# Moving the third and fourth quarter of w_out into the first pass, and x's second reading ahead of w_in

## The chip, the cores and the metric

The kernel runs on one core of one Trainium2 chip. The metric is the time of one execution on the device in microseconds (us); lower is better. The core has TensorE (PE in the rows; its weight loads are PEld), VectorE (DVE), ScalarE (ACT), GpSimd (POOL) and SyncE (SP), which issues nearly all DMAs. Each engine works through its own instructions in the order in which the program writes them.

## What is computed

The input x has 8 sequences of 3072 tokens with 256 channels. Three stages follow one another:

```python
X = np.fft.fft(np.fft.fft(x, axis=1), axis=2).real          # 24576 tokens x 256
logits = X @ phi                                            # soft mixture of 8 experts, 32 slots
d = softmax of logits over all tokens; c = softmax over slots
slot_input = d.T @ X                                        # 32 x 256
slot_out[e] = np.maximum(slot_input[e] @ w1[e], 0) @ w2[e]  # w1: 8 x 256 x 1024, w2: 8 x 1024 x 256
Y = c @ slot_out
h = Y @ w_in                                                # w_in: 256 x 2048
out = (s * np.maximum(h, 0)**2 + b) @ w_out                 # w_out: 2048 x 256
```

w_in and w_out are float64 in memory; the kernel turns them into float32 itself.

## The kernel before, in words

**The stages.** The *first pass* reads x once, turned, in 24 pages of 1 MB (`load_x`, three to a sequence) and computes the logits' Fourier sums: `emit_v` (L381) multiplies a page with the projected table on TensorE into `vt`, ScalarE or VectorE copies that to `vts`, `turn_v` (L412) transposes it and copies it to `v`, and `emit_t` (L426) makes `tps` (for the last sequence `tpa` and `tpb`), which ScalarE copies to `tt`. For the last but one sequence these eight copies are put aside in `late_t` and written out after `emit_t`. Then come the logits (`lp`, L571), their maximum, the exponentials `dt` and `hp` (L651). The *second pass* (L829 on) reads x again in another order, 24 pages `xrt` (`load_xr`), and sums `slot_input` in `racc` (L726), two pages to a step, while VectorE, GpSimd and ScalarE make the second softmax (`c_steps`). Then the experts use w1 (L925) and w2 (L957), and last the feed-forward blocks (L1121, L1151, L1154), which make up most of the time.

**Pages.** The loaded tiles and several others live in pages of 8 KB per partition: 15 in `ring`, three and two more behind the first pass, two more in the second. `page` takes one and `drop` gives it back; a DMA into a page waits until its former content has been read. SP issues in order, so a load that waits holds up all loads behind it.

**w_out and w_in.** Each is loaded in four chunks of 1 MB. `wo_load(k)` (L194) takes a page for the raw float64 numbers, and for every second chunk also a page `wo` for float32 and a page `whl` for the two float16 parts that the blocks use. Its work is a list of small steps: four integer steps on VectorE (L154 to L166), a product (L174), a maximum (L224), four bias adds on GpSimd (L283), a scale (L206, L207) with two casts on ScalarE (L214), and two low parts on VectorE (L218), which wait for the casts. The raw page is given back with the product, the `wo` page with the odd chunk's last low part. `wi_load(k)` does the like for w_in with the first steps and the maximum.

**Who orders it.** Everything is written out by hand in one order per engine. A planner keeps rough times in `at` while it writes: `pump_a` (L320) takes loads from the string `ORDER` (x: a page of the first reading, w: a chunk of w_out, r: a page of the second reading, l and h: tables) as long as enough pages are free, and `fill` writes the small steps in where it believes VectorE to be idle:

```python
def fill():
    while side_step(at["pe"] + 0.7):
        pass
```

`side_step(0.0, True)` writes the next small step whatever the planner believes. Behind the first pass the loads stand in the list `todo`, and `pump` takes the next one when it has the pages it asks for (first entry of its tuple; third entry: that many in the first two pools).

Of the kernel before, what the change touches and what calls it, by code (L numbers as in the profile page):

```python
# [9 lines left out]
F16 = mybir.dt.float16  # L10
# [22 lines left out]
def tile_fft2__then__softmoe__then__act_relu2(  # L33
# [19 lines left out]
    P = 128  # L53
# [53 lines left out]
    todo = []  # L107
# [19 lines left out]
    def side_step(limit, any_time=False):  # L127

        met = set()
        for n, (c, lag, f, cost) in enumerate(side_work):  # L130
            start = max(at["dve"], side_at[c] + lag)
            if c not in met and (any_time or start < limit):
                side_work.pop(n)
                f()
                at["dve"] = side_at[c] = start + cost
                return True
            met.add(c)
        return False
# [53 lines left out]
    wo_rest = []  # L192

    def wo_load(k):  # L194
        if k % 2 == 0:
            t, kk = page([P, 8, D], F32, "wo")
            wo.append(t)
            wok.append(kk)
            whl.append(page([P, 8, 2, D], F16, "whl", 2)[0])
# [5 lines left out]
        def scale():  # L205
            nc.vector.tensor_scalar(out=top, in0=top, scalar1=1e-30, scalar2=1.0 / WMAX, op0=ALU.max, op1=ALU.mult)  # L206
            nc.vector.reciprocal(inv, top)  # L207
            if k < 2:
                cast()
# [18 lines left out]
        rest = [(0.0, lambda j=j: low(j), 0.65) for j in range(2)]  # L228
        if k > 1:
            steps[4:4] = wo_rest  # L230
            wo_rest[:] = [(0.0, cast, 0.0), *rest]
        else:
            steps += rest
# [3 lines left out]
    def wi_load(k):  # L237
# [9 lines left out]
        steps[4:4] = wo_rest  # L247
        wo_rest.clear()
# [55 lines left out]
    ORDER = "xxxwxxxxxxwxxxxxxxxxxxrllhhrr"  # L304
# [69 lines left out]
    with tc.tile_pool(name="xtp", bufs=1, side="right") as xtp, tc.tile_pool(name="vp", bufs=1, side="right") as vp, \  # L374
# [136 lines left out]
        while side_step(0.0, True):  # L511
            pass
        turn_v(2 * B - 2)
        emit_v(2 * B - 1)
        turn_v(2 * B - 1)
        nc.gpsimd.tensor_copy(ltabs[0][0][64:P], ltabs[0][0][0:64])
        nc.gpsimd.tensor_copy(ltabs[1][0][64:P], ltabs[1][0][0:64])
        emit_t(B - 1)
        load_xr()
# [291 lines left out]
    todo += [(1, load_xr)] * (left - 8)  # L811
    for k in (2, 3):
        todo += [(5 - 2 * (k - 1), doubles.pop(0)[1], 3 - k), (1, load_xr)]
    for k in range(4):
        todo += [(2 - k % 2, lambda k=k: wi_load(k), 1 - k % 2), (1, load_xr)]
    todo += [(1, load_xr)] * 2
# [18 lines left out]
    for n in range(NST + 2):  # L835
# [13 lines left out]
        for _ in range(2 if n >= 5 else 1 if n == 4 else 0):  # L849
            side_step(0.0, True)  # L850
        c_until(CR * n + CR / 2)
        for _ in range(2 if n >= 6 else 1 if n >= 4 else 0):
            side_step(0.0, True)
# [456 lines left out]
```

## Time and profile before

| | before |
|---|---|
| median of 3 runs | 1399.15 us (1397.02 to 1400.8) |
| the profiled execution | 1397.21 us, its span 1395.4 us |
| TensorE busy | 98% of the span |
| VectorE / ScalarE / GpSimd busy | 84% / 73% / 17% |

The profiled execution is one run; its span reaches from the first to the last instruction of the program, and 1.8 us of its time lie around the span. It lies 1.9 us below the median. All times below count from the span's start. A row of a timeline tells start, length, engine, line, operation and tiles of a group of like instructions, and in brackets how long the engine was idle before it and what released it.

### The profile page before, as it was taken

The numbers are of one execution on the slowest core, as the hardware profiler recorded it, in microseconds if no ns is written. First come the engines' busy times: TensorE is split into PE (matmuls) and PEld (weight loads), VectorE is DVE, ScalarE is ACT, GpSimd is POOL, SyncE is SP. The second block draws the span as 40 slices with busy tenths as digits, with TensorE's granted clock in tenths as the row PEclk, the third lists the DMA queues.
The fourth block names the chain that finished last, engine by engine and source line by source line (L and its number), as shares of the span: only waits on it lengthen the run. The fifth ranks groups of instructions, "written<-read, shape, count | busy, mean of one in ns | idle before, by whom it ended". The sixth has DMA issues, their size and how long they took to land.

```text
span 1395.4 us, 23097 instructions
## 1 busy us (share of the span) xinstructions
PE 1374.5 (98%) x9036; PEld 841.0 (60%) x9036; DVE 1165.6 (84%) x1477; ACT 1014.8 (73%) x1436; POOL 234.0 (17%) x287
## 2 busy tenths in 40 slices
PE   8989989999999999999999999999999999999998
PEld 6767545566666666666666666666666666666665
DVE  2447946998989898989899998989898989888886
ACT  2767325877778777778777777777777777777775
POOL 1227100121212121212121211111111111111110
PEclk9999999999999999999999999999999999999999
DMA  9997991101010101010101101010101010101000
GB/s 353 417 318 310 403 410 56 36 24 37 23 37 20 36 20 37 23 37 20 37 23 30 30 23 34 23 35 22 36 24 33 23 36 24 37 23 33 24 21 30
DMA packets 72382, 112.28 MB, mean 80 GB/s; under 512 B 33904, under 2 KB 59632, under 8 KB 64976
## 3 DMA queue, kind: packets, MB, share of 16 engines
q1 hardware_dynamic: 72144, 110.70, 23.2%
q8 instruction: 71, 1.16, 0.4%
q14 instruction: 39, 0.32, 0.1%
q0 software_dynamic: 128, 0.10, 0.0%
HBM read 78.48 MB, written 25.17 MB: 74 GB/s over the span
## 4 chain that ended last, share of the span: by engine, by line
PE 90%; DMA 8%; DVE 1%; SPq 1%; ACT 0%; issue 0%; ACTq 0%; DVEq 0%
PE op L1151 47%; PE op L1154 24%; PE fhp L1121 12%; DMA xb<-in_x_turned_dram 4%; PE racc L726 3%; DMA w2t<-in_moe_w_dram 1%; DMA xrt<-in_x_pages_dram 1%; DMA htab_t<-in_htab_dram 1%; PE vt L401 1%; PE hp L651 1%; PE dps L711 1%; PE eop L957 1%; SPq L1084 0%; PE tps L454 0%; DVE r L1127 0%
## 5 line engine op out<-in xcount | busy, mean ns | idle before, releaser
L1151 PE MATMUL op<-whl,rhl 128*128 128x512 f16 x3072 | 1025.3, 379 | 0.8 <-ACT rhl L1111 0.6
L1154 PE MATMUL op<-whl,rhl 128*128 128x256 f16 x3072 | 835.7, 273 | 0.0
L1126 ACT ACTIVATE r<-fhp,wsc 128x768 f32<-128x768 f32 (+1 forms) x513 | 461.4, 900 | 230.5 <-PE fhp L1121 229.4
L1127 DVE SCALAR_TENSOR_TENSOR r<-fhp,r 128x768 f32<-128x768 f32 (+1 forms) x513 | 488.5, 952 | 113.8 <-ACT r L1126 103.7
L1112 DVE TENSOR_TENSOR rhl<-r,rhl 128x768 f16<-128x768 f32 x511 | 506.2, 991 | 0.9 <-ACT rhl L1111 0.9
L1151 PEld LDWEIGHTS <-rhl 128*128 128x128 f16 x3072 | 300.5, 98 | 335.6 <-ACT rhl L1111 0.9
L1111 ACT CAST rhl<-r 128x768 f16<-128x768 f32 x511 | 420.2, 822 | 1.8 <-DVE r L1127 1.8
L1154 PEld LDWEIGHTS <-rhl 128*128 128x128 f16 x3072 | 300.6, 98 | 62.5 <-issue 0.3
L1166 POOL TENSOR_TENSOR ot<-ot,bias 128x256 f32<-128x256 f32 x189 | 137.7, 729 | 974.6 <-DVE ot L1164 974.6
L1121 PE MATMUL fhp<-ct,g 128*128 128x384 f16 x1024 | 250.5, 326 | 1.1 <-DMA g<-gs 0.8
L1121 PEld LDWEIGHTS <-g 128*128 128x128 f16 x1024 | 99.9, 98 | 69.0 <-issue 1.1
L1163 ACT ACTIVATE o<-op,small 128x256 f32<-128x256 f32 x189 | 89.6, 475 | 16.7 <-PE op L1154 16.7
L1164 DVE SCALAR_TENSOR_TENSOR ot<-op,small,o 128x256 f32<-128x256 f32 x192 | 91.6, 477 | 0.3
L401 PE MATMUL vt<-xb,phd 128*64 128x512 f32 (+3 forms) x288 | 48.8, 479 | 1.9 <-DMA xb<-in_x_turned_dram 1.8
L726 PE MATMUL racc<-xrt,dh 128*64 128x256 f32 x384 | 44.3, 382 | 0.7 <-ACT dh L716 0.7
L423 DVE COPY v<-vq 128x512 f32<-128x512 f32 (+1 forms) x15 | 8.4, 594 | 39.9 <-PE vq L419 39.9
L401 PEld LDWEIGHTS vt<-xb,phd 128*64 128x64 f32 x288 | 27.3, 139 | 20.8 <-issue 10.8
L726 PEld LDWEIGHTS racc<-xrt,dh 128*64 128x64 f32 x384 | 26.4, 137 | 21.2 <-issue 7.5
L468 ACT COPY tt<-tps 32x512 f32<-32x512 f32 x48 | 27.7, 576 | 6.5 <-PE tps L454 6.0
L410 ACT COPY vts<-vt 128x512 f32<-128x512 f32 (+1 forms) x15 | 8.0, 536 | 30.3 <-PE vt L401 30.1
L773 POOL TENSOR_TENSOR lg<-lg,rm 112x512 f32<-112x512 f32 x16 | 22.9, 1435 | 3.3 <-DVE rm L771 3.3
L755 POOL TENSOR_TENSOR lg<-et,lg 112x512 f16<-112x512 f32 x16 | 18.6, 1160 | 0.5 <-ACT lg L758 0.5
(230 smaller groups left out, 504.9 us busy)
## 6 DMA issues: line engine op xcount, KB each, us to landing
xb<-in_x_turned_dram SPq DMA_DIRECT2D x24, 1024.0 KB, 20.2
xrt<-in_x_pages_dram SPq DMA_DIRECT2D x24, 1024.0 KB, 13.8
out_dram<-ot SPq DMA_DIRECT2D x128, 128.0 KB, 1.7
w1t<-in_moe_w_dram SPq DMA_DIRECT2D x8, 1024.0 KB, 17.7
out_dram<-ot SPq DMA_DIRECT2D x128, 64.0 KB, 2.0
raw<-in_moe_w_out_dram SPq DMA_DIRECT2D x4, 1024.0 KB, 13.7
raw<-in_moe_w_in_dram SPq DMA_DIRECT2D x4, 1024.0 KB, 11.5
w2t<-in_moe_w_dram SPq DMA_DIRECT2D x4, 1024.0 KB, 19.3
```

What stands on the lines that cost most here:

```text
L401: nc.tensor.matmul(vt[64 * h:64 * h + 64, o:o + k, :], lhsT=phd[:, c, sg, :], rhs=turned(pg, c, i, k, rev), start=(c == 0 and m < 2), stop ...
L726: nc.tensor.matmul(raccs[acc][64 * h:64 * h + 64, :], lhsT=dh[:, m, g].rearrange("p j e -> p (j e)"), rhs=xr[k][0][:, g, t, :], start=(sum ...
L1111: nc.scalar.copy(a, r2)
L1112: nc.vector.tensor_tensor(out=l, in0=r2, in1=a, op=ALU.subtract)
L1121: nc.tensor.matmul(hp[k * split][:, k, :].rearrange("p (s b m) -> p s b m", s=2, b=B), lhsT=g16[:, f * P:(f + 1) * P], rhs=c, start=True, ...
L1126: nc.scalar.activation(out=r[:, k], in_=hp[i][:, k], func=AF.Relu, scale=wsc[:, 2, p:p + 1])
L1127: nc.vector.scalar_tensor_tensor(out=r2[:, k], in0=hp[i][:, k], scalar=0.0, in1=r[:, k], op0=ALU.max, op1=ALU.mult)
L1151: nc.tensor.matmul(op.rearrange("p h d -> p (h d)"), lhsT=a, rhs=w.rearrange("p h d -> p (h d)"), start=(f == 0), stop=False)
L1154: nc.tensor.matmul(op[:, 0, :], lhsT=l, rhs=w[:, 0, :], start=False, stop=(f == NFC - 1))
L1163: nc.scalar.activation(out=o1, in_=op[:, 1, :], func=AF.Copy, scale=qv)
L1164: nc.vector.scalar_tensor_tensor(out=ot, in0=op[:, 0, :], scalar=qv, in1=o1, op0=ALU.mult, op1=ALU.add)
L1166: nc.gpsimd.tensor_tensor(out=ot, in0=ot, in1=bias, op=ALU.add)
```

## The change

The third chunk of w_out is loaded in the first pass ahead of x's last four pages, the fourth behind x's last page, in place of one page of the second reading; in the second pass all remaining pages of x but four come ahead of w_in. `whl` may now lie in any pool. `side_step` gets a bound `below` on the chunk. The third chunk's casts come with its scale, the fourth's as a step of their own; the list `wo_rest`, which had delayed them, is gone. At the end of the first pass only steps of the first three chunks are written out where all were; the fourth chunk's steps follow one, two and two at three later places, and the last six in steps 1 and 2 of the second pass, where w_in's begin at step 6.

```diff
@@ -124,10 +124,12 @@
 
     side_at, raws, doubles = {}, [0], []
 
-    def side_step(limit, any_time=False):
+    def side_step(limit, any_time=False, below=9):
 
         met = set()
         for n, (c, lag, f, cost) in enumerate(side_work):
+            if c >= below:
+                continue
             start = max(at["dve"], side_at[c] + lag)
             if c not in met and (any_time or start < limit):
                 side_work.pop(n)
@@ -189,14 +191,12 @@
         for _ in range(k):
             nc.tensor.matmul(t, lhsT=ones[:, :t.shape[0]], rhs=ones[:, :t.shape[1]], start=True, stop=True)
 
-    wo_rest = []
-
     def wo_load(k):
         if k % 2 == 0:
             t, kk = page([P, 8, D], F32, "wo")
             wo.append(t)
             wok.append(kk)
-            whl.append(page([P, 8, 2, D], F16, "whl", 2)[0])
+            whl.append(page([P, 8, 2, D], F16, "whl")[0])
         w = wo[k // 2][:, 4 * (k % 2):4 * (k % 2) + 4, :]
         hl = whl[k // 2][:, 4 * (k % 2):4 * (k % 2) + 4]
         d = w.rearrange("p k d -> p (k d)")
@@ -205,7 +205,7 @@
         def scale():
             nc.vector.tensor_scalar(out=top, in0=top, scalar1=1e-30, scalar2=1.0 / WMAX, op0=ALU.max, op1=ALU.mult)
             nc.vector.reciprocal(inv, top)
-            if k < 2:
+            if k < 3:
                 cast()
 
         def cast():
@@ -225,12 +225,9 @@
             out=top, in_=d.rearrange("p (a n) -> p a n", a=2), axis=AX.X, op=ALU.max, apply_absolute_value=True), 1.15))
         steps.append((0.0, lambda: bias_add(k, d.rearrange("p (k d) -> p k d", d=D)), 0.0))
         steps.append((0.0, scale, 0.35))
-        rest = [(0.0, lambda j=j: low(j), 0.65) for j in range(2)]
-        if k > 1:
-            steps[4:4] = wo_rest
-            wo_rest[:] = [(0.0, cast, 0.0), *rest]
-        else:
-            steps += rest
+        if k == 3:
+            steps.append((0.0, cast, 0.0))
+        steps += [(0.0, lambda j=j: low(j), 0.65) for j in range(2)]
         side_at[k] = dma_ready()
         side_work.extend((k, *f) for f in steps)
 
@@ -244,8 +241,6 @@
         steps = double_steps(d, w_in[c * P:(c + 1) * P, 1024 * h:1024 * h + 1024], False)
         steps.append((0.0, lambda: nc.vector.tensor_reduce(
             out=wim4[:, k:k + 1], in_=d, axis=AX.X, op=ALU.max, apply_absolute_value=True), 1.15))
-        steps[4:4] = wo_rest
-        wo_rest.clear()
         side_at[4 + k] = dma_ready()
         side_work.extend((4 + k, *f) for f in steps)
 
@@ -301,7 +296,7 @@
     CR = 1.5
     WARM = 4
     LEAD, TOL, LT, LX, HX = 14.0, 0.5, 0, 0, 1
-    ORDER = "xxxwxxxxxxwxxxxxxxxxxxrllhhrr"
+    ORDER = "xxxwxxxxxxwxxxxxxxwxxxxwllhhrr"
     tpool = tc.alloc_tile_pool(name="tpool", bufs=1)
     doubles += [((3, 1, 3, 1)[k], lambda k=k: wo_load(k)) for k in range(4)]
 
@@ -508,14 +503,19 @@
         emit_t(B - 2)
         for f in late_t:
             f()
-        while side_step(0.0, True):
+        while side_step(0.0, True, 3):
             pass
         turn_v(2 * B - 2)
+        side_step(0.0, True)
         emit_v(2 * B - 1)
         turn_v(2 * B - 1)
+        for _ in range(2):
+            side_step(0.0, True)
         nc.gpsimd.tensor_copy(ltabs[0][0][64:P], ltabs[0][0][0:64])
         nc.gpsimd.tensor_copy(ltabs[1][0][64:P], ltabs[1][0][0:64])
         emit_t(B - 1)
+        for _ in range(2):
+            side_step(0.0, True)
         load_xr()
         keep_warm(psv.tile([P, 4 * P], F32, tag="vt", name="warm", bufs=2)[:, :P], WARM)
         for i in range(2):
@@ -808,12 +808,9 @@
         nc.sync.dma_start(out=w2t[e][:, c], in_=w2[e].rearrange("(p c) d -> p c d", p=P)[:, c])
 
     left = NS1 - len(xr) - sum(t[1] is load_xr for t in todo)
-    todo += [(1, load_xr)] * (left - 8)
-    for k in (2, 3):
-        todo += [(5 - 2 * (k - 1), doubles.pop(0)[1], 3 - k), (1, load_xr)]
+    todo += [(1, load_xr)] * (left - 4)
     for k in range(4):
         todo += [(2 - k % 2, lambda k=k: wi_load(k), 1 - k % 2), (1, load_xr)]
-    todo += [(1, load_xr)] * 2
     todo += [(1, lambda e=e: w1_load(e)) for e in range(8)] + [(1, lambda e=e: w2_load(e)) for e in range(4)]
     parts2 = [(e, 0) for e in range(4, 8)] + [(4, 3), (5, 3), (6, 3), (7, 1), (7, 4), (7, 5)]
     todo += [(h == 0, lambda e=e, h=h: w2_load(e, h)) for e, h in parts2]
@@ -846,10 +843,10 @@
             r_sum(n - 2, dhs[n - 2], 0)
         busy("dve", 0.6)
         c_until(CR * n)
-        for _ in range(2 if n >= 5 else 1 if n == 4 else 0):
+        for _ in range(2 if n > 5 or n in (1, 2) else 0):
             side_step(0.0, True)
         c_until(CR * n + CR / 2)
-        for _ in range(2 if n >= 6 else 1 if n >= 4 else 0):
+        for _ in range(2 if n > 5 else n in (1, 2)):
             side_step(0.0, True)
         at["pe"] += 4.9
         if n >= 2:
```

## Rows read from the trace of the kernel before

**Rows 1.** Stages: busy us (instructions) per engine, granted clock, DMA share, GB/s.

```profile
57.90:83.20 25.30, 25.30 (x175) 17.26 (x174) 5.02 (x9) 19.71 (x36) 4.40 (x4) 1.00 1.02 341
...
83.20:89.30 6.10, 3.86 (x86) 3.21 (x84) 2.43 (x4) 4.85 (x12) 4.56 (x4) 1.00 1.04 209
...
121.00:149.40 28.40, 27.08 (x222) 15.50 (x223) 23.38 (x38) 12.14 (x24) 18.32 (x18) 1.00 0.79 291
...
202.00:208.00 6.00, 2.89 (x24) 1.08 (x26) 0.21 (x1) 0.77 (x2) 0.00 (x0) 0.83 1.01 406
...
224.00:1395.40 1171.40, 1165.53 (x7170) 700.76 (x7166) 1047.51 (x1288) 909.91 (x1235) 180.83 (x227) 1.00 0.11 29
```

**Rows 2.** Timeline of PE from 186 to 222 us, the second expert matrix.

```profile
206.41 3.37 PE L957 MATMUL eop<-w2t,hT 128*32 128x256 f32 x26 [1.90 <-DMA w2t<-in_moe_w_dram]
...
210.29 1.93 PE L957 MATMUL eop<-w2t,hT 128*32 128x256 f32 x32
...
215.39 2.52 PE L957 MATMUL eop<-w2t,hT 128*32 128x256 f32 x32
```

**Rows 3.** Timeline of SP: issues at 141 and 208 us.

```profile
141.73 0.33 SPq L333 DMA_DIRECT2D xrt<-in_x_pages_dram  x1
...
208.95 0.33 SPq L808 DMA_DIRECT2D w2t<-in_moe_w_dram  x1
```

**Rows 4.** Issues at 126, 141 and 208 us: KB, us to landing.

```profile
xrt<-in_x_pages_dram SPq DMA_DIRECT2D x1, 1024.0 KB, 5.0
...
xrt<-in_x_pages_dram SPq DMA_DIRECT2D x1, 1024.0 KB, 7.6
...
w2t<-in_moe_w_dram SPq DMA_DIRECT2D x1, 128.0 KB, 7.7
```

**Rows 5.** What SP waited for until 240 us: total us, times, longest.

```profile
SPq L333 <- PE racc L726: 24.4, 8, 5.0
```

**Rows 6.** SP's issues of x from 46.8 to 54.9 us, and their landing.

```profile
46.86 7.81 SPq L296 DMA_DIRECT2D xb<-in_x_turned_dram  x4
...
xb<-in_x_turned_dram SPq DMA_DIRECT2D x4, 1024.0 KB, 20.0
```

**Rows 7.** Timeline of all engines at the end of the first pass.

```profile
74.83 3.65 PE L401 MATMUL vt<-xb,phd 128*64 128x512 f32 x16
...
80.50 4.69 ACT L466 COPY tt<-tps 32x512 f32<-32x512 f32 x8 [1.04 <-PE tps L454]
...
80.83 2.38 PE L401 MATMUL vt<-xb,phd 128*64 128x384 f32 x20
...
80.94 0.69 DVE L423 COPY v<-vq 128x512 f32<-128x512 f32 x1 [5.24 <-PE vq L419]
...
83.33 0.56 DVE L410 COPY vts<-vt 128x384 f32<-128x384 f32 x1 [1.70 <-PE vt L401]
...
83.94 0.55 PE L419 MATMUL vq<-ident,vts 128*128 128x128 f32 x3 [0.73 <-DVE vts L410]
...
85.07 1.16 PE L432 MATMUL tpa<-f_sb,v 128*128 128x128 f32 x8 [0.58 <-DVE v L423]
...
86.27 2.98 ACT L436 COPY tt<-tpa 32x256 f32<-32x256 f32 x8 [1.08 <-PE tpa L432]
...
89.30 0.97 PE L571 MATMUL lp<-tt,ltab 64*64 64x128 f32 x13 [0.93 <-ACT tt L436]
```

**Rows 8.** Chunk steps: ns of one, shortest, median and longest.

```profile
L214 ACT ACTIVATE whl<-wo,wsc x8: 705/722/737, 38.7 to 162.9; 128x512 f16<-128x512 f32 x8
...
L218 DVE SCALAR_TENSOR_TENSOR whl<-wo,wsc,whl x8: 742/746/753, 39.5 to 163.8; 128x512 f16<-128x512 f32 x8
...
L166 DVE TENSOR_SCALAR raw<-raw x8: 689/689/691, 32.6 to 182.9; 128x1024 uint32<-128x1024 uint32 x8
```

**Rows 9.** Timelines of ACT and POOL early in the second pass.

```profile
128.90 0.64 ACT L769 ACTIVATE lg<-lg 112x512 f32<-112x512 f32 x1
...
145.20 3.47 POOL L283 TENSOR_TENSOR bias<-bias,wo 128x256 f32<-128x256 f32 x4 [5.79 <-DVE wo L174]
```
## The prediction

> **What bounds the kernel now.** I read busy time by stage first, then who waits in the stages that are not full: TensorE's timeline, SP's issues and waits, the end of the first pass. From 224 us to the end TensorE is busy for 1165.5 of 1171.4 us [rows 1]: the feed-forward blocks run back to back, so whatever moves their start moves the end one for one. The change touches nothing behind that point; the question is when the blocks start.
>
> Before 224 us, TensorE has three faces. In the first pass, 57.9 to 83.2 us, it has no idle time at all [rows 1]. In the second pass it is nearly full too. But from 202 to 208 us it works 2.89 of 6 us [rows 1]: the second matrix of the experts (L957) waits for w2t, and its last group ends at 215.39 + 2.52 = 217.9 us [rows 2]. The last piece of w2 was issued at 208.95 us and landed 7.7 us later, at 216.65 [rows 3, 4]. So **the end of the loads** releases the blocks, 1.25 us before the last group ends.
>
> At the end the loads run without a gap, at 406 GB/s; from 121 to 149.4 us they move only 291 [rows 1]. There SP waits for pages: L333 stood behind racc 8 times, 24.4 us in all [rows 5]. All 20 pages are held: one whl, four of lg, fifteen of xr, and racc frees them one by one. Chunk 2 of w_out then asks for three at once (wo, whl, raw), and the DMA engines stand still while they collect. That is the gain on offer: bring the two chunks in earlier, and let x's pages follow one freed page at a time.
>
> **The change, part by part.** *Loads of the first pass.* Chunk 2 enters ahead of x's pages 20 to 23, chunk 3 behind them, and one page of the second reading leaves. Eight loads are outstanding and each takes 20.0 us to land [rows 6], so x's last page, issued at 46.86 + 7.81 - 0.33 = 54.34, lands at 74.3, and now some 2.6 later, about 77. Its matmuls start at 80.83 [rows 7]. Page 22 moves from 71.8 to about 74.5; its batch starts at 74.83 [rows 7]. Cost nothing, with 0.3 us to spare at page 22: the cover is that TensorE runs late here, not the loads. ltab and htab shift by the same 2.6 us net and have more slack than that.
>
> *Chunk 2's steps on DVE.* Followed through the planner's own sums (costs 0.65 and 1.15 us, limit `at["pe"] + 0.7`), the four integer steps, the product and the maximum are emitted in batch 6 and fit into DVE's idle time before 74 us. The bias adds, the scale with its two casts, and the two low parts do not meet the limit; they are left for the drain, which stands *behind* the late copies of tt. ACT runs in order: those eight copies take it from 80.50 to 85.19 [rows 7]. Then come two casts of 0.72 us, and DVE's low parts wait for them [rows 8]. And DVE runs in order: behind the low parts stands the copy of v (80.94 before), then chunk 3's first step, then vts (83.33 before) [rows 7].
>
> Step by step: first cast ends 85.19 + 0.72 = 85.9; two low parts of 0.75 each, 87.4; v 0.69, 88.1; chunk 3's first step 0.69 [rows 8], 88.8. Neighbours on DVE overlap a little in the records, so vts starts near 88.7 instead of 83.33: **+5.3 us**. vts releases three transposes, those a copy, that the eight tpa matmuls, those ACT's eight copies, and those the logits at 89.30, with no slack anywhere in that string [rows 7]. Logits, exponentials, hp and racc follow one another without waiting for a load, so the second pass starts 5.3 us late.
>
> *TensorE's clock.* Between vt's end at 83.2 and the transposes TensorE would now do nothing for some 6 us. Where it waited from 202 us on, the granted clock of 202 to 208 us was 0.83, and 26 of L957's matmuls took 3.37 us where 32 took 1.93 afterwards [rows 1, 2]. From 83.2 to 89.3 us, with shorter waits, the clock stayed 1.00 [rows 1]. If the half level (1.2 of 2.4 GHz) meets the transposes (0.55 us) and tpa (1.16 us) [rows 7], they double: +1.7 us. The bounds are 0 and 1.7; the new wait is as long as the one that brought the clock down, so I take **+1.7**, 7.0 us together. The Trainium skill (TensorE: Matmul & The Clock Gate, HAM oscillation) says that a wait for data long enough throttles the array and lets the next work start cold; that speaks against this change, and by it the sum has the +1.7, without it not.
>
> *Chunk 3's other steps.* Its second and third stand after v's last copy, the fourth and fifth after tt's; each pair fits where DVE waits for TensorE or ACT. Cost 0; without that cover up to 2 us.
>
> *Loads of the second pass.* Relative to a second pass that starts on time: of the 20 pages seven are now held by two whl, one wo and four lg, thirteen by xr. What has been asked for by then is the same 17 MB: thirteen of xr and four chunks, where it was fifteen and two. The next page of x (number 13) goes out when racc frees page 0, as one does now; with nothing ahead of it that takes 5.0 us to land [rows 4]. Number 14 takes wo's page, free when DVE has done chunk 3's second low part. That stands behind the cast, and the cast behind ACT's exponential at 128.90 + 0.64 [rows 9]: 129.55 + 0.72 + 0.72, and 0.75 for the low part, gives 131.8, about when racc frees page 1 anyway. It lands at 131.8 + 5.0 = 136.8. From there pages come free faster than loads land. What is left is 29 MB: nine pages of x, four of w_in, 16 of the experts. Before, the page of x issued at 141.73 landed 7.6 later, at 149.35 [rows 3, 4], and the 26 MB behind it ended at 216.65: 2.59 us each. 29 x 2.59 = 75.1, so the loads would end at 211.9 instead of 216.65: **-4.8 us** on a second pass in time. But every one of these pages is freed by racc, so a pass 7.0 us late makes it 218.9.
>
> *Also moved.* DVE loses the two chunks' work in the second pass (some 15 us, off the path). The bias adds, 3.47 us on POOL [rows 9], now stand ahead of one subtraction of lg; ACT reaches that exponential no earlier anyway. w_in's maximum is taken in the second pass instead of among the experts, under 1 us of TensorE's and not on the loads' path.
>
> **Sum.** +5.3 + 1.7 - 4.8 = +2.2 us. TensorE on its own, without the 3.1 us that it idled from 202 to 208 us and the 1.8 us that the clock cost it there (3.37 - 26/32 x 1.93) [rows 1, 2], would end its last group at 217.9 - 4.9 + 7.0 = 220.0; the loads allow 218.9 + 1.25 = 220.1. Both arrive together. On the profiled execution (1397.2 us, 1.9 below the median of 1399.15) that gives 1399.4; on the median, 1401.4. I say **1401.0**.
>
> **Rivals.** A measurement of this kernel tells about 0.3%, 4.2 us, from no change.
>
> *The low parts don't wait* (chance 0.10). If chunk 2's casts get onto ACT ahead of the late copies, for instance because a step falls under the planner's limit after all, neither 5.3 nor 1.7 is paid and -4.8 is left: 1394.4. For it: DVE has room before 74 us. Against it: the drain is written behind those copies, and ACT cannot pass them.
>
> *The clock holds* (inside the forecast). Without the 1.7: +0.5, 1399.7.
>
> *The second pass's loads hang on chunk 3's last low part* (chance 0.20). SP issues in order; page 14 waits for wo's page, and every load behind it waits with it. Scale, cast and low parts cross DVE, ACT and DVE again amid the rows' softmax, and POOL's 3.47 us of bias adds stand ahead of the subtraction that feeds ACT's exponential at 128.90 [rows 9]. Each us that the low part ends after 131.8 (plus the shift of the pass) is a us at the end; it decides from 2.0 us on, where the sum passes 4.2. At 3.5 us later: +5.7, 1404.9. For it: three engines in a chain. Against it: DVE waits for ACT there anyway.
>
> *The loads gain nothing* (chance 0.08). If the first pass has too few of its 15 pages free, chunk 3 and the tables are issued late, the order of landing is much as before, and gain and delay are both smaller: about 1399.5.
>
> **How the numbers follow.** The forecast's balance has 0.62: 1398 to 1404 by the clock's bounds and 1 us on each load term. Faster by over 0.3% is the first rival, 0.10. Slower is the third with the forecast's upper edge, 0.23. Within 0.3% is the rest, 0.67. The range reaches from 1396.0 to 1405.5; it leaves out most of the first rival and the far end of the third.
>
> **What would show it.** Right: ACT's late tt copies, then two whl casts, then DVE's two low parts directly ahead of v's copy near 87 us; vts near 88.7; the logits at 94.5 to 96.5 instead of 89.3; a lowered clock around 88 to 93 us; no third-page wait of raw behind racc in the second pass, and page 13 and 14 of x issued near 133 and 139 us; the last w2t piece landing near 219. Wrong: v's copy still near 81 us with low parts ahead of it, or TensorE waiting in racc for ACT, or the last piece of w2t landing before 214 us although the logits came late; then pages were not what held the loads.

## The result and the profile after

The changed kernel takes 1407.56 us (median of 6 runs, 1406.69 to 1409.29), the kernel before beside it 1398.63: ratio 1.0067, 95% interval 1.0054 to 1.0080. It is slower by 8.9 us, where the forecast was 1401.0 and the range ended at 1405.5. The profiled execution took 1406.83 us with a span of 1405.1; before it was 1397.21 and 1395.4, so what follows accounts for 9.7 us. Of all executions below one, of experiment 10, took 2409.4 us at a granted clock of 0.56; no ratio counts it.

The stages of the changed kernel (columns as in [rows 1]):

```profile
83.20:99.00 15.80, 6.21 (x91) 5.06 (x87) 10.00 (x11) 6.71 (x15) 7.63 (x7) 0.68 1.01 273
...
134.90:201.80 66.90, 62.46 (x521) 35.68 (x523) 40.11 (x56) 19.00 (x37) 15.61 (x16) 0.97 0.93 367
201.80:227.50 25.70, 25.42 (x283) 13.24 (x277) 5.07 (x16) 7.71 (x9) 1.15 (x2) 0.93 0.82 322
...
233.80:1405.10 1171.30, 1165.36 (x7169) 700.71 (x7166) 1047.19 (x1288) 910.21 (x1235) 181.26 (x227) 1.00 0.11 29
```

The feed-forward part is as long as before (1171.4 us [rows 1] and 1171.3; from the last expert group's end to the end of the span 1177.5 and 1177.7): everything happened ahead of it. Between the first pass and the logits, where TensorE had 3.86 us of work in 6.1 [rows 1], it now has 6.21 in 15.8, at a mean clock of 0.68. From 201.8 to 227.5 us, where the experts had waited for w2t, it is now full.

In the first pass TensorE now stands for a page of x where it had no idle time before [rows 1]; the page was issued directly behind the third chunk's load and landed at 70.2 us:

```profile
70.31 2.37 PE L396 MATMUL vt<-xb,phd 128*64 128x384 f32 x20 [0.46 <-DMA xb<-in_x_turned_dram]
```

The end of the first pass, timelines of ACT, of DVE, of GpSimd (POOL) and of TensorE, in that order (start us, us, engine, line, operation, tiles, count, idle time before):

```profile
81.03 4.69 ACT L461 COPY tt<-tps 32x512 f32<-32x512 f32 x8 [1.03 <-PE tps L449]
85.75 1.33 ACT L214 ACTIVATE whl<-wo,wsc 128x512 f16<-128x512 f32 x2
...
86.50 2.79 DVE L218 SCALAR_TENSOR_TENSOR whl<-wo,wsc,whl 128x512 f16<-128x512 f32 x2 [10.00 <-ACT whl L214]
89.22 0.68 DVE L418 COPY v<-vq 128x512 f32<-128x512 f32 x1
89.82 1.85 DVE L156 TENSOR_SCALAR wo<-raw 128x1024 uint32<-128x1024 uint32 x1
91.59 0.54 DVE L405 COPY vts<-vt 128x384 f32<-128x384 f32 x1
...
86.20 1.89 POOL L514 COPY ltab<-ltab 64x2048 f32<-64x2048 f32 x1 [10.10 <-DMA ltab<-in_ltab_dram]
89.23 1.89 POOL L515 COPY ltab<-ltab 64x2048 f32<-64x2048 f32 x1 [1.14 <-DMA ltab<-in_ltab_dram]
...
92.18 0.90 PE L414 MATMUL vq<-ident,vts 128*128 128x128 f32 x3 [8.44 <-DVE vts L405]
93.67 2.08 PE L427 MATMUL tpa<-f_sb,v 128*128 128x128 f32 x8 [0.58 <-DVE v L418]
...
99.03 4.61 PE L571 MATMUL lp<-tt,ltab 64*64 64x128 f32 x125 [0.59 <-ACT tt L431]
```

The string that the prediction wrote down is there: ACT's eight late copies, two casts, DVE's two low parts, v, the fourth chunk's first step, vts. But two of its links are longer than their rows of before: two low parts take 2.79 us where one took 0.746 [rows 8], the first step 1.85 where such a step took 0.69. Beside them run GpSimd's two copies of ltab, which in the kernel before ran at 82.41 and 85.21 us, beside no step of a chunk. vts starts 8.26 us later than before (83.33 to 91.59), TensorE's transposes and tpa run at the half level (0.90 and 2.08 us for 0.55 and 1.16 [rows 7]), and lp starts at 99.03 instead of 89.30.

The second pass and the experts, timeline of TensorE:

```profile
189.59 0.37 PE L259 MATMUL mx<-ident,small 128*1 128x128 f32 x1 [4.14 <-DVE small L255]
...
206.75 3.27 PE L922 MATMUL ehp<-w1t,si 128*32 128x512 f32 x16
...
217.97 1.93 PE L954 MATMUL eop<-w2t,hT 128*32 128x256 f32 x32
...
225.52 1.93 PE L954 MATMUL eop<-w2t,hT 128*32 128x256 f32 x32
```

In racc TensorE stands 4.14 us for the transpose of w_in's maximum, because DVE has not finished w_in's last chunk. In the kernel before that transpose ran among the experts:

```profile
195.06 0.27 PE L264 MATMUL mx<-ident,small 128*1 128x128 f32 x1 [0.31 <-DVE small L260]
```

There are two more spells at the half level, with a granted clock of 0.50: one from 189.0 us, still within that stand, to 192.4, and one from 206.1 to 209.5, in which one expert group took 3.27 us for 1.92. The second is no steady part of the change: in the profiles of experiments 1, 4 and 5, which have the stand too, it is missing, and racc's end to the last expert group's end is 23.98 us. The four groups of L954 then run without a wait for w2t, and the last ends at 227.45.

The stretches of TensorE rest on these rows: hp, the first and the last rows of racc, in the kernel before and then in the changed one.

```profile
106.14 14.51 PE L651 MATMUL hp<-htab_t,dt 112*128 112x104 f32 x128 [0.22 <-DMA xrt<-in_x_pages_dram]
124.48 1.95 PE L726 MATMUL racc<-xrt,dh 128*64 128x256 f32 x16 [0.73 <-ACT dh L716]
180.43 5.40 PE L726 MATMUL racc<-xrt,dh 128*64 128x256 f32 x48
...
116.56 14.51 PE L651 MATMUL hp<-htab_t,dt 112*128 112x104 f32 x128 [0.21 <-ACT dt L668]
134.89 1.95 PE L726 MATMUL racc<-xrt,dh 128*64 128x256 f32 x16 [0.72 <-ACT dh L716]
196.44 5.40 PE L726 MATMUL racc<-xrt,dh 128*64 128x256 f32 x48
```

lp's start: +9.73; lp to hp 16.84 before, 17.53 now; first racc 124.48 before, 134.89 now (+10.4); first racc to racc's end 61.35 before, 66.95 now (+5.6); racc's end to the last expert group's end 32.1 before, 25.6 now (-6.5). 10.4 + 5.6 - 6.5 = +9.5, nearly the whole difference of the spans. The last piece of w2 was issued at 216.40 and landed 8.4 us later, at 224.8:

```profile
216.40 0.33 SPq L808 DMA_DIRECT2D w2t<-in_moe_w_dram  x1
...
w2t<-in_moe_w_dram SPq DMA_DIRECT2D x1, 128.0 KB, 8.4
```

So 89.9 us after first racc, where it was 216.65 - 124.48 = 92.2. The loads did gain; TensorE lost more.

### The profile page after: what moved, and what is told of

The parts are those of the page before. It is cut to its first block, busy times and chain, and to the rows that moved or that the text cites. A ratio compares the mean times of both kernels' runs of the same rounds, so it can differ in the third digit from the quotient of the medians.

```text
span 1405.1 us, 23093 instructions
## 1 busy us (share of the span) xinstructions
PE 1373.8 (98%) x9036; PEld 840.4 (60%) x9036; DVE 1166.8 (83%) x1477; ACT 1015.4 (72%) x1436; POOL 234.5 (17%) x287
## 3 DMA queue, kind: packets, MB, share of 16 engines
q8 instruction: 71, 1.16, 0.3%
## 4 chain that ended last, share of the span: by engine, by line
PE 91%; DMA 4%; DVE 3%; ACT 1%; issue 1%; SPq 1%; DVEq 0%; ACTq 0%
PE op L1148 46%; PE op L1151 24%; PE fhp L1118 12%; DMA xb<-in_x_turned_dram 4%; PE racc L726 2%; PE vt L396 1%; PE hp L651 1%; PE ehp L922 1%; PE dps L711 1%; PE eop L954 1%; SPq L1081 0%; PE lp L571 0%; PE tps L449 0%; DVE wi L160 0%; DVE wi L176 0%
## 5 line engine op out<-in xcount | busy, mean ns | idle before, releaser
L396 PE MATMUL vt<-xb,phd 128*64 128x384 f32 (+3 forms) x288 | 49.3, 479 | 4.7 <-DMA xb<-in_x_turned_dram 4.7
L405 ACT COPY vts<-vt 128x512 f32<-128x512 f32 (+1 forms) x15 | 8.0, 536 | 30.8 <-PE vt L396 30.6
## 6 DMA issues: line engine op xcount, KB each, us to landing
w1t<-in_moe_w_dram SPq DMA_DIRECT2D x8, 1024.0 KB, 14.8
```

The lines of the kernel that those rows point to most:

```text
L396: nc.tensor.matmul(vt[64 * h:64 * h + 64, o:o + k, :], lhsT=phd[:, c, sg, :], rhs=turned(pg, c, i, k, rev), start=(c == 0 and m < 2), stop ...
```

## The experiments

Executions differ by some us in when x's first page lands and so in all later starts, so traces are compared by stretches, and times by medians of runs beside the kernel before.

**1. The drain ahead of the late copies.**

```diff
         emit_t(B - 2)
+        while side_step(0.0, True, 3):
+            pass
         for f in late_t:
             f()
-        while side_step(0.0, True, 3):
-            pass
```

> The changed kernel with the drain of the third chunk's steps written ahead of the late copies of tt. Theory (two stalls of TensorE made the loss, one behind DVE's low parts at the end of the first pass, one for w_in's maximum in the second): the casts run on ACT near 80 us, the copy of v near 82.5, vts near 83.9, the granted clock stays 1.00 and the logits start near 90.5 instead of 99.0. The wait for w_in's maximum stays (3 to 6 us in racc). Time near 1399, 8 us below the changed kernel. Rival (the loads' end sets the time, the stalls only took the place of waits for w2t): TensorE waits for w2t again and the time falls by 3 us at most, 1404 or more.

1401.96 us, ratio to before 1.0023 (1.0011 to 1.0034): 5.6 us less than the changed kernel. Timeline of DVE:

```profile
82.12 1.41 DVE L218 SCALAR_TENSOR_TENSOR whl<-wo,wsc,whl 128x512 f16<-128x512 f32 x2 [4.15 <-ACT whl L214]
83.45 0.68 DVE L418 COPY v<-vq 128x512 f32<-128x512 f32 x1
86.53 0.69 DVE L156 TENSOR_SCALAR wo<-raw 128x1024 uint32<-128x1024 uint32 x1 [2.40 <-DMA raw<-in_moe_w_out_dram]
...
89.98 2.79 DVE L164 SCALAR_TENSOR_TENSOR wo<-raw,wo 128x1024 uint32<-128x1024 uint32 x1
```

The low parts come 4.4 us earlier and take 1.41 us, and from the end of vt to lp it takes 9.2 us for 15.3: the cause of the largest term is shown. What was not foreseen stands next: the fourth chunk's first step, ahead of vts, now waits 2.40 us for its data, and a later step meets GpSimd's copies (2.79 us). So lp starts at 94.39, where 90.5 was expected, and the granted clock, expected at 1.00, was 0.50 at 90 us. The time missed the expected 1399 by 3.

**2. No early maximum of w_in.**

```diff
-        if not side_work and len(wi) == 2 and raws[0] == 0 and len(wim_steps) > 1 and n <= NST:
-            wim_steps.pop(0)()
```

> The changed kernel without the steps of w_in's maximum in the second pass; they are taken among the experts. Theory: logits at 99.0 as in the changed kernel, no wait of 4 us for DVE inside racc and no lowered clock behind it, racc ends near 196 instead of 201.8, the last w2t piece lands near 221 and then decides; time 1402 to 1404, 4 to 5 us below the changed kernel. Rival (loads set the time): w2t still lands near 224.7, TensorE waits for it, time 1407.

1404.12 us, ratio 1.0037 (1.0025 to 1.0050): 3.4 us less than the changed kernel, where 4 to 5 were expected. The wait in racc is gone, and TensorE waits for w2t again, 0.57 us within the last group. In the profiled execution GpSimd's copies came later, at 90.70 us, and DVE's low parts, unedited, took 1.41:

```profile
88.46 1.41 DVE L218 SCALAR_TENSOR_TENSOR whl<-wo,wsc,whl 128x512 f16<-128x512 f32 x2 [10.00 <-ACT whl L214]
```

So which of DVE's steps the copies meet differs between executions. The stand in racc does not: in all profiles with the early maximum (changed, experiments 1, 4 and 5) racc took 66.95 to 69.10 us, in those without it 61.3, and 62.35 in experiment 8.

**3. Both edits:** the two diffs above together.

> Both edits: drain ahead of the late copies, w_in's maximum among the experts. Theory: logits near 90.5, no wait in racc, racc ends near 187, the last w2t piece lands near 214 instead of 216.6 in the kernel before; time 1395 to 1397, 2 to 3 us below the kernel before: what the loads alone were worth. Rival (the pages give the loads nothing): the last w2t piece lands at 216.5 or later, time 1398.6 or more.

1401.22 us, ratio 1.0013 (1.0000 to 1.0025): missed by 4 us; the rival's time and landing (222.8 us) came. The two gains do not add, 6.3 us for 5.6 and 3.4. A likely reason, not tried alone: with lp earlier the last w2t decides, and a stand of TensorE's ahead of it costs little. And the fourth chunk still stood in the way, as in experiment 1: its first step held DVE 2.37 us for raw, the next two took 2.94 and 2.79 beside GpSimd ahead of the last copies of tt.

**4. ltab's copies on ACT instead of GpSimd** (the changed kernel otherwise).

```diff
-        nc.gpsimd.tensor_copy(ltabs[0][0][64:P], ltabs[0][0][0:64])
-        nc.gpsimd.tensor_copy(ltabs[1][0][64:P], ltabs[1][0][0:64])
+        nc.scalar.copy(ltabs[0][0][64:P], ltabs[0][0][0:64])
+        nc.scalar.copy(ltabs[1][0][64:P], ltabs[1][0][0:64])
```

> The changed kernel with the two copies of the ltab tables on ACT instead of POOL (ACT is idle there). Theory (POOL's two copies stretch DVE's two low parts from 1.4 to 2.8 us and the fourth chunk's first step from 0.69 to 1.85): low parts 1.4 us together, first step 0.7, the copy of v near 87.9, vts near 89.1, logits 2.5 us earlier, near 96.5; time 2 to 3 us below the changed kernel. Rival (they are slow for another reason, such as a cold or shared memory port of DVE or the transfers under way): both stay at 2.8 and 1.85.

A single execution, 1405.7 us, 1.9 below the changed kernel's median; a time that alone shows nothing. Timeline of DVE, the instructions shown above for the changed kernel:

```profile
88.17 1.41 DVE L218 SCALAR_TENSOR_TENSOR whl<-wo,wsc,whl 128x512 f16<-128x512 f32 x2 [10.00 <-ACT whl L214]
89.50 0.68 DVE L418 COPY v<-vq 128x512 f32<-128x512 f32 x1
90.11 0.68 DVE L156 TENSOR_SCALAR wo<-raw 128x1024 uint32<-128x1024 uint32 x1
```

1.41 for 2.79 and 0.68 for 1.85: 2.55 us of vts's delay in the changed kernel's profile were GpSimd's copies. The clock fell as before (transposes 0.90 us, tpa 2.08).

**5. TensorE kept busy in the gap.**

```diff
         emit_v(2 * B - 1)
+        keep_warm(psv.tile([P, 4 * P], F32, tag="vt", name="warm", bufs=2)[:, :P], 40)
         turn_v(2 * B - 1)
```

> The changed kernel with 40 further warm-up matmuls (on ones, into a buffer of the size of vt) between the last slice's matmuls of x and its transposes, where TensorE otherwise stands while DVE finishes the third chunk. Theory: the granted clock of 0.50 from 86.6 to 96.9 us is what made the last transposes take 0.90 us instead of 0.55 and tpa 2.08 instead of 1.16; with TensorE busy in the stand the clock stays 1.00, these rows go back, lp starts 1.3 to 2 us earlier and the time is 1405.5 to 1406.5 us. Rival: the first TensorE work behind DVE's vts copy is on time anyway, or ACT's copies of tpa are bound elsewhere: the clock stays up but the time is 1407 to 1408 as for the changed kernel. Second rival: the additional matmuls stand themselves ahead of the transposes and cost what they save.

1404.99 us, ratio 1.0049 (1.0031 to 1.0067): 2.6 us less. Timeline of TensorE:

```profile
84.38 9.20 PE L192 MATMUL warm<-ones 128*128 128x128 f32 x80
93.41 0.49 PE L414 MATMUL vq<-ident,vts 128*128 128x128 f32 x3
94.49 1.16 PE L427 MATMUL tpa<-f_sb,v 128*128 128x128 f32 x8 [0.58 <-DVE v L418]
```

The clock stays at 1.00 from 84 to 99.3 us and both rows are back at full speed: that the clock had made them long is shown. What this is worth is not. The matmuls on ones also stood ahead of the transposes (vts was done at 90.3, the transposes began at 93.41), so both the theory and the second rival hold, and from the end of vt to lp it takes 14.8 us for 15.3. The other differences lie where nothing was edited: lp to hp 16.57 us for 17.53, racc's end to the last expert group's end 23.98 for 25.6. And the interval of the ratio overlaps that of the changed kernel; one of the ten executions took 1417.3 us.

**6. The fourth chunk's five steps behind the last copies of tt** (with both edits of 3).

```diff
-        side_step(0.0, True)
         emit_v(2 * B - 1)
         turn_v(2 * B - 1)
-        for _ in range(2):
-            side_step(0.0, True)
...
         emit_t(B - 1)
-        for _ in range(2):
+        for _ in range(5):
             side_step(0.0, True)
```

> As the run with both edits (drain of the first three chunks ahead of ACT's late copies, no early maximum of w_in), and the five written steps of the fourth chunk moved behind the last slice's tt copies. Theory: in the run with both edits the fourth chunk's first step held DVE for its raw chunk's landing (2.37 us), and the two following held the copies of tt (tpb) by 5.7 us; with them behind these copies lp starts about 3 us earlier, first racc 2 to 3 us earlier, and the time is 1398 to 1399.5 us against 1401.2. Rival: the lp stage is bound by DVE's work, so that the same steps cost as much behind the copies as ahead of them: first racc and time unchanged, 1400.5 to 1401.5.

1400.45 us, ratio 1.0011 (1.0000 to 1.0022), close to the rival. Timelines of TensorE, then DVE:

```profile
89.92 3.05 PE L568 MATMUL lp<-tt,ltab 64*64 64x128 f32 x82 [0.93 <-ACT tt L431]
97.42 7.63 PE L568 MATMUL lp<-tt,ltab 64*64 64x128 f32 x174 [4.46 <-DVE cm L583]
...
89.40 0.69 DVE L156 TENSOR_SCALAR wo<-raw 128x1024 uint32<-128x1024 uint32 x1
90.13 2.86 DVE L160 SCALAR_TENSOR_TENSOR wo<-raw,wo 128x1024 uint32<-128x1024 uint32 x1
```

lp starts 6.0 us behind the end of vt, where it was 6.1 in the kernel before. Then TensorE stands 4.46 us for DVE's reductions, which stand behind 7.3 us of chunk steps (89.40 to 96.65). lp to hp takes 21.4 us where it took 16.84. DVE has no room there: what is not paid ahead of tt is paid in lp.

**7. The fourth chunk's load behind ltab's** (otherwise as 6).

```diff
-    ORDER = "xxxwxxxxxxwxxxxxxxwxxxxwllhhrr"
+    ORDER = "xxxwxxxxxxwxxxxxxxwxxxxllwhhrr"
```

> As the run before it (fourth chunk's steps behind the last copies of tt), and the fourth chunk's load behind the two loads of ltab instead of ahead of them. Theory: with the raw chunk ahead, ltab lands later, so that GpSimd's copies of ltab move onto DVE's copies of v and tt of the last slice (in the kernel before they start at 82.4 and 85.2 us, in the run with both edits at 88.7 and 91.1); with ltab first they start some 2.6 us earlier, and the last copies of tt take their time alone: lp and the time another 0.5 to 1.5 us earlier, 1397 to 1398.5 us, no slower than the kernel before. Rival: ltab is not on the path and only htab's loads come later: time as in the run before it, or up to 1 us longer.

1402.07 us, ratio 1.0019 (1.0010 to 1.0028): no gain, if anything a loss. x's last page now stood directly ahead of ltab's loads and landed late, 25.6 us after its issue instead of 20; TensorE stood 1.63 us for it (more below, experiment 11).

**8. All the fourth chunk's steps in the second pass** (otherwise as 6).

```diff
         emit_t(B - 1)
-        for _ in range(5):
-            side_step(0.0, True)
...
-        for _ in range(2 if n > 5 or n in (1, 2) else 0):
+        for _ in range(2 if n > 5 or n in (0, 1, 2) else 0):
...
-        for _ in range(2 if n > 5 else n in (1, 2)):
+        for _ in range(2 if n > 5 or n in (0, 1, 2) else 0):
```

> As the run with the fourth chunk's steps behind the last copies of tt, with all eleven of that chunk's steps in the first three steps of the second pass instead; its load stays at the end of the first pass. Theory: in the run before, its five steps took DVE from 89.40 to 96.65 us, TensorE's logits matmuls stood 4.46 us for DVE's reductions, and first racc came 4.6 us later relative to the start of lp; on DVE in the second pass they cover nothing. First racc then comes at 125 to 125.5 us, the end of racc 4 to 5 us earlier than in that run, the last of w2t lands at 214 to 216 us, and the time is 1395 to 1397.5 us, faster than the kernel before (1398.7). Rival: the loads at the end are bound by what they move and not by the pages that racc returns, or the raw page, held some 30 us longer, delays the second pass's x: the last w2t lands at 217 or later and the time is 1398 to 1400.

1402.14 us, ratio 1.0021 (1.0012 to 1.0030): the rival's late landing, and a time 2 us above its range. TensorE no longer waited for DVE in lp (lp to hp still took 19.6 us, 3.00 of them put down to "issue"), but the stretch from first racc to the last w2t is 92.5 us, as long as before the change. What SP waited for (us in total, times, longest):

```profile
SPq L794 <- PE racc L721: 16.9, 3, 13.7
```

One load of w1 waited 13.7 us for a page that racc freed shortly before its end. Before that, one load of x had waited 3.6 us for a low part (1.0 in experiment 6) and another 2.3 for the product that frees raw. With raw's page held into the second pass the pages come round in another order; which of these waits costs the 4 us was not tried.

**9. Only the order of x and w_in** (the kernel before otherwise).

```diff
-    todo += [(1, load_xr)] * (left - 8)
+    todo += [(1, load_xr)] * (left - 6)
...
-    todo += [(1, load_xr)] * 2
```

> The kernel before with one part of the change alone: the last two x pages of the second reading go ahead of w_in's chunks in the order of loads (third and fourth chunk of w_out stay in the second pass). Theory: the order of loads alone is worth little, since SP waits for pages that the same steps of racc return, and the last w2t lands where it did (216.6 us) within 1 us: 1397.5 to 1399.5 us. Rival: the order is what the change's better use of the loads rests on (in the prediction's terms -4.8 us for the loads on time): 1394 to 1396 us. Second rival: w_in's maximum comes later and holds TensorE, above 1400 us.

1400.12 us, ratio 1.0006 (0.9998 to 1.0015): within what can be told from no change. First racc to the last w2t: 92.4 us. The order alone gains the loads nothing, and w_in's maximum did not come into racc (61.34 us). In this execution lp ran slowly though nothing of it is edited (windows, then timeline of TensorE):

```profile
101.00:106.00 5.00, 4.51 (x25) 4.11 (x25) 2.59 (x5) 1.46 (x7) 0.00 (x0) 0.51 1.01 421
...
95.20 4.71 PE L571 MATMUL lp<-tt,ltab 64*48 64x128 f32 x127 [1.92 <-issue]
```

A wait that nothing in the profile explains, then the half level: lp to hp 20.9 us for 16.84. A single trace can carry some us of this, so its lp stage is not a measure by itself.

**10. The third chunk alone in the first pass,** drained ahead of the late copies; the fourth stays in the second pass, order as before.

```diff
-    ORDER = "xxxwxxxxxxwxxxxxxxwxxxxwllhhrr"
+    ORDER = "xxxwxxxxxxwxxxxxxxwxxxxrllhhrr"
...
-    todo += [(1, load_xr)] * (left - 4)
+    todo += [(1, load_xr)] * (left - 7)
+    todo += [(1, doubles.pop(0)[1]), (1, load_xr)]
```

> Of the change only the third chunk's part: it is loaded in the first pass, and its steps are written ahead of ACT's late copies; the fourth chunk stays in the second pass, w_in and x in the order of the kernel before, no early maximum of w_in. Theory: the third chunk's steps lie under TensorE's work of the first pass, so that lp and first racc start as in the kernel before (within 1 us beside what the first x landing shifts them), and DVE's cost is nothing; the second pass has one load of 1 MB (2.5 us) less, of which the last w2t shows 1 to 2.5 us: 1396 to 1398 us, against 1399 before. Rival: the order in which pages come free sets the last w2t, not the number of loads: the gap from racc's end to the last w2t stays at 30.8 us and the time is 1398.5 to 1400.

1400.86 us, ratio 1.0011 (1.0001 to 1.0020): the rival, at a time 0.9 us above its range. First racc to the last w2t: 93.8 us, and from racc's end to it 32.5, where 30.8 would have been no gain. One load fewer in the second pass brings nothing by itself.

**11. Both chunks three x pages earlier** than in the change, all their steps ahead of the late copies (otherwise as 6, without its five steps).

```diff
-    ORDER = "xxxwxxxxxxwxxxxxxxwxxxxwllhhrr"
+    ORDER = "xxxwxxxxxxwxxxxwxxxxwxxxllhhrr"
...
-        while side_step(0.0, True, 3):
+        while side_step(0.0, True):
```

> Both chunks in the first pass as in the change, but three and seven x pages earlier (the third behind x's page 16, the fourth behind page 20 in the order of loads), so that all their steps, the fourth's too, are done under TensorE's work on x and ahead of ACT's late copies; nothing of them is left for the lp stage or the second pass; no early maximum of w_in. Theory: DVE has 1.1 us of work in 10 between 60 and 80 us in the kernel before, so the fourth chunk's steps, which in the lp stage cost 4.6 us, cost nothing there; x's last page lands 5 us later than before, which leaves TensorE about 1 us of slack; first racc comes 0 to 2 us later than in the kernel before beside the shift of the first x page, the stretch from first racc to the last w2t is 3 to 4 us shorter than before's 92.14, and the time is 1396 to 1398 us, faster than the kernel before (1399). Rival: x's last pages come too late for TensorE, lp starts 2 us or more later, and the time is 1399 to 1401.

1402.53 us, ratio 1.0032 (1.0019 to 1.0044): the rival, 1.5 us above its range. x's last page, its issue and landing, and TensorE's wait for it (DMA issues of 60.5 us; timeline of TensorE):

```profile
xb<-in_x_turned_dram SPq DMA_DIRECT2D x1, 1024.0 KB, 25.8
...
86.36 4.07 PE L393 MATMUL vt<-xb,phd 128*64 128x384 f32 x20 [2.27 <-DMA xb<-in_x_turned_dram]
```

It landed at 86.3 us, 7.5 after the page ahead of it, where pages follow each other by 2.5. (The fourth chunk, too, went three pages earlier, not seven as the expectation has it.) The fourth chunk's steps cost nothing here, lp to hp took 16.3 us, and first racc to the last w2t 90.8, 1.4 us less than before, where 3 to 4 were expected. The loads of the first pass paid: lp starts at 96.46.

**12. As 6, with ltab's copies on ACT behind its copies of tt.**

```diff
-        nc.gpsimd.tensor_copy(ltabs[0][0][64:P], ltabs[0][0][0:64])
-        nc.gpsimd.tensor_copy(ltabs[1][0][64:P], ltabs[1][0][0:64])
         emit_t(B - 1)
+        nc.scalar.copy(ltabs[0][0][64:P], ltabs[0][0][0:64])
+        nc.scalar.copy(ltabs[1][0][64:P], ltabs[1][0][0:64])
```

> As the run with the fourth chunk's steps behind the last copies of tt (1400.45 us), with the two copies of ltab moved from GpSimd to ACT, behind ACT's copies of tt; nothing else runs on GpSimd beside DVE's five steps but the clearing of htab's tiles. Theory: two of the five steps stood at 2.86 and 1.22 us for 1.23 and 0.69 alone because GpSimd's copies ran beside them; without these the five take 5.1 instead of 7.3 us, TensorE's stand in lp falls from 4.46 us to some 2.5, first racc comes some 2 us earlier relative to the start of lp, and the time is 1398 to 1399.5 us. Rival: ACT's copies (1.9 us each) hold the copies of lp on ACT instead, and the time stays at 1400 to 1401.5; or GpSimd's clearing of htab takes the copies' place beside DVE, and the steps stay as long.

1398.23 us, ratio 1.0003 (0.9994 to 1.0012): level with the kernel before, 9.3 us under the changed kernel. Timelines of TensorE and DVE, then the last issue of w2:

```profile
95.88 7.54 PE L568 MATMUL lp<-tt,ltab 64*64 64x128 f32 x171 [1.71 <-DVE cm L583]
...
128.11 1.95 PE L723 MATMUL racc<-xrt,dh 128*64 128x256 f32 x16 [0.73 <-ACT dh L713]
...
90.48 1.23 DVE L160 SCALAR_TENSOR_TENSOR wo<-raw,wo 128x1024 uint32<-128x1024 uint32 x1
91.74 1.27 DVE L164 SCALAR_TENSOR_TENSOR wo<-raw,wo 128x1024 uint32<-128x1024 uint32 x1
92.89 0.96 DVE L168 TENSOR_SCALAR raw<-raw 128x1024 uint32<-128x1024 uint32 x1
...
208.29 0.33 SPq L805 DMA_DIRECT2D w2t<-in_moe_w_dram  x1
...
w2t<-in_moe_w_dram SPq DMA_DIRECT2D x1, 128.0 KB, 7.8
```

The step that took 2.86 us takes 1.23; the five end after 5.4 us instead of 7.3, the stand in lp is 1.71 instead of 4.46, and lp to hp is 19.5. These durations show what GpSimd's copies did; the times of experiments 6 and 12 alone do not, as the intervals overlap. The last piece of w2 lands 208.29 + 7.8 - 128.11 = 88.0 us after first racc. This is the best form of the change that was found, and its gain and its cost are level.

## Why the prediction was wrong

**The bound** was right: everything lies ahead of the experts' end, and the rest moved with it one for one.

**The loads of the first pass, cost 0 with 0.3 us to spare:** mis-sized, if little. TensorE stood 0.46 us at 70.31 for the page of x behind the third chunk's load. Such a stand, of 0.46 to 1.42 us, is in nine of the eleven profiles that load the third chunk there, and neither in the kernel before nor in experiment 9; in experiment 11, with the load three pages earlier, it comes at 63.1 us.

**Low parts behind the casts, +5.3:** right, and shown by experiment 1. ACT's late copies end at 85.72, the casts and the low parts follow, in the order named.

**The length of that string:** wrong. The step "two low parts of 0.75 each ... chunk 3's first step 0.69" took durations from stretches in which no such GpSimd copy ran beside them. vts came 8.26 us later; without the 0.5 us by which the first pass ended later in this execution that is 2.4 more than 5.3. Experiment 4 shows where they went: GpSimd's copies of ltab, which the prediction did not mention, add 1.4 and 1.2 us; experiment 12 shows the same for the steps in lp. The Trainium skill (SBUF — State Buffer, SBUF: two separate sides) says that DVE and GpSimd share one pair of ports which one instruction holds for its whole length, against DVE's instructions with two inputs in SBUF (if GpSimd's reads SBUF) or in a fast mode. The trace agrees: a copy of 1.89 us began at 86.20, the first low part at 86.50, and the pair ended 1.4 us late, where standing until the copy's end would make 1.6.

**The clock, +1.7:** right. vts to lp took 5.97 us before and 7.44 now, +1.5. TensorE stood from 83.74 to 92.18 us, and the granted clock was 0.50 from 86.6 to 96.9. The Trainium skill (TensorE: Matmul & The Clock Gate, HAM oscillation) says that a wait for data that is long enough throttles the array, and the next work starts cold. The trace agrees, with 0.90 and 2.08 us for 0.55 and 1.16, and experiment 5 holds the clock at 1.00 by keeping TensorE busy.

**Chunk 3's other steps, cost 0:** wrong in kind; in the changed kernel itself no cost is shown. Two of the five stood ahead of DVE's first reduction of lp, and lp to hp grew by 0.7 us, but in experiment 5, with the same steps there, it took 16.57 us, less than before. Their price shows where they follow each other in lp: TensorE stood 4.46 us for DVE in experiment 6 (7.3 us of steps) and 1.71 in experiment 12 (5.4 us), and lp to hp was 4.6 and 2.7 us longer. The cover that I named, DVE's waits for TensorE or ACT, is thin in lp, where DVE is busy 11.82 of 15.2 us in the kernel before.

**w_in's maximum, "under 1 us of TensorE's and not on the loads' path":** the step that failed most. The prediction priced TensorE's work for it and not a wait. The maximum is written out where no small step is left (`if not side_work and ...`); with the two chunks gone from the second pass, that is while racc still runs (so the code reads; it was not tried apart). DVE finishes w_in's chunks only at 189.4 us, and the transpose of the maximum stands in TensorE's queue ahead of the last two groups of sums. It cost 4.14 us of standing and a spell at the half level: racc grew by 5.6 us. Taken away, 3.4 us come back (experiment 2).

**The loads of the second pass, -4.8:** right in direction, and too large for the changed kernel. From first racc to the last w2t: 92.2 us before; 89.9 changed, and 90.5, 89.4 and 89.0 in experiments 1, 4 and 5, all with the stand in racc; without it 87.9, 90.6, 88.8, 87.4, 90.8 and 88.0 in experiments 2, 3, 6, 7, 11 and 12. That is -2.3 in the changed kernel and -1.4 to -4.7 in all; what sets it within these bounds is not shown. Experiments 9 (92.4) and 10 (93.8) show that neither the order nor the third chunk alone gives it; in experiment 8 (92.5), with raw's page held into the pass, it is gone.

**The sum.** The forecast was 6.6 us low. The maximum is 3.4 of that, by medians. GpSimd's copies are 2.55 in the profiled execution; as they meet other steps in the profiles of experiments 2 and 5, their share of the median is not shown. The string of two delays behind ACT's late copies was read rightly; that the loads balance it was not so.

The rival with slower at its end (loads hanging on the fourth chunk's last low part) came about only in small. Page 14 of x waited for racc and landed at 146.88 us, where the prediction had 136.8 and the pass is 10.4 late. Page 15, issued at 143.48, waited 1.1 us for the low part, below the 2.0 from which the rival was to decide (what SP waited for):

```profile
SPq L328 <- DVE whl L218: 1.1, 1, 1.1
```

What stays open: the part of the 6.6 us that the maximum does not explain, as far as GpSimd's copies do not either; why the lp stage varies by up to 4 us between executions of the same code (the waits put down to "issue"), and whether the pages could be given out so that experiment 8 gains.

## What to carry to other kernels

When work is moved, list for its new place what runs on every engine beside it, not only what is queued ahead: a duration is only good for the neighbours that it was measured with. A step that only "moves earlier" can make another step, placed by a condition such as "when nothing is left", appear where its data are not ready; follow each such condition through the new order. And before paying for a gain at the bound, ask what slack pays for it: here loads left the second pass, which they held up, for the first pass and the lp stage, where DVE had none to spare.

## What the runs showed of the hardware

Beside a GpSimd copy of ltab (1.89 us alone, up to 2.70 beside DVE's steps in experiment 1) DVE's two-input steps of 128 x 1024 grew from 1.23 to as much as 2.94 us, two low parts from 1.41 to 2.79, and a one-input step on integers from 0.69 to 1.85; DVE's copies out of PSUM (0.68) did not grow. Beside GpSimd's clearing of htab (MEMSET, whose rows name no input) a two-input step took 1.23 to 1.27 us, and a one-input step 0.96 for 0.69 (experiment 12).

The last load of 1 MB ahead of ltab's four loads of 256 KB landed late in each of four traces, whichever load it was: 4.6 us after the one ahead of it in the kernel before (a page of the second reading), 5.1 in the changed one (the fourth chunk), 6.9 and 7.5 in experiments 7 and 11 (x's last page), where 2.5 is usual. Why is not shown. Here the place just ahead of such tables is one for a load that nobody waits for.
